# Two row-tiled matmul streams in one gated two-layer network: the upper stream's second products first, both streams started and ended together

## The chip, the core and the metric

The kernel runs on one core of one Trainium2 chip. The metric is the device time of one execution in microseconds (us). TensorE is called PE in the profile (its weight loads PEld), VectorE DVE, ScalarE ACT, GpSimd POOL, and the queue that issues most transfers SP.

## The reference

A causal 7-tap convolution with softmaxed taps for each of 8 heads is followed by two layers `x @ w_in`, a gate, `@ w_out`. All is float32; there are 8192 tokens, 192 features and 2048 hidden features.

```python
w = exp(weight - max); w = w / (sum(w) + 1e-9)               # 8 heads x 7 taps
x = conv(x, w)                                              # (2, 4096, 192) -> (8192, 192)
h = x @ w_in1;  x = (h * clip(h + 3, 0, 6) / 6) @ w_out1     # layer 0, (192, 2048), (2048, 192)
h = x @ w_in2;  out = where(h > 0, h, exp(min(h, 0)) - 1) @ w_out2   # layer 1
```

## The kernel before

**Blocks and slots.** The tokens are cut into 16 blocks of 512 (256 of each of the two batch rows), features and hidden features lie on partitions, and tokens run along the free axis. One slot `(l, b, f)` is layer `l`, block `b` and 128 of the 2048 hidden features, so a block has 16 slots in a layer and the kernel 512. The list `slots` fixes their order: blocks 0 and 1 of layer 0 woven into each other, blocks 2 to 6 of layer 0, then a block of layer 1 and a block of layer 0 in turn (nine of each), and at the end blocks 9 to 15 of layer 1 alone.

**A slot's work.** `mm1` makes the first products `h = w_in.T @ x` in PSUM (tile `h`, pool `ps_h` with three banks). `gate` reads `h`: in layer 0 ACT writes `u = relu(h + 3)` and DVE `g = min(u, 6) * h`; in layer 1 ACT writes `u = relu(-h)` and `u = exp(-u)`, and DVE `g = max(u - 1, h)`. `split_g` makes a high part `gh` (ACT) and a low part `gl = g - gh` (DVE). `mm2` makes the second products, which add to two accumulators of the block, `p0` and `p1`: high weights by `gh` and low weights by `gh` into `p0`, both at once into `p1`, then both with `gl`, five products in all. ACT and DVE take a slot in the order `u`, (`exp`,) `gh` of the slot before, and `g`, `gl` of the slot before (`first_done`), then side work: `run_jobs` steps through the convolution of later blocks, the preparation of weights and the stores, spread by costs and due times.

**Two streams.** The first 36 slots (`BOTH + LAG`) run first products on all 128 rows of the array. After that each product is cut in two: the lower 64 rows (`LO`) and the upper 64 rows (`UP`) of the contraction are two products in two row tiles of the array, which run at the same time. `stream(half, ...)` writes the two instruction lists, and a loop takes one instruction of each in turn. In each stream slot `s` has its first products (five or four, alternating) and then the five second products of slot `s - 4` (`LAG`). The lower stream is 8 instructions ahead (`BEHIND`): `h` is begun by the lower stream and ended by the upper one, and a tiny GpSimd write (`relay`) tells the upper that the lower has left the bank. So 8 lower products run alone at the start, and 8 upper ones at the end. Slots 32 to 511 have split second products, slots 36 to 511 split first products.

**Accumulators.** Each stream has its own `p0` and `p1`, so four of the five banks of `ps_o` are in use within a block, and the next block begins with one free bank. Where a block's lower products end, ACT copies them out (`lower_sum`: `y0`, `s1`), which frees their banks; where its upper ones end, DVE adds them to that (`upper_sum`, `job`). At such an end `stream` gives out the gate of the upper stream's slot after the first DVE sum. The last block is summed, transposed on PE and stored by `last_store`; `finish` orders its second products so that the last slot's come last.

Of the kernel before, what the change touches and what calls it, by code (L numbers as in the profile page):

```python
# [8 lines left out]
F32 = mybir.dt.float32  # L9
# [4 lines left out]
ALU = mybir.AluOpType  # L14
# [2 lines left out]

P = 128
LAG = 4
BEHIND = 8  # L20
PAUSE = 2
RA = 7
STAG = 2
LEAD = 1
# [5 lines left out]
NB = 512  # L30
HB = NB // 2
# [24 lines left out]
def conv_moe_moe2(ctx: ExitStack, tc: tile.TileContext, x, weight, w_in1, w_out1, w_in2, w_out2, out):  # L56
# [18 lines left out]
    B, S, D = x.shape  # L75
# [3 lines left out]
    NF = FF // P  # L79
# [6 lines left out]
    NBLK = NT // NB  # L86
# [267 lines left out]

    rests = {}

    def lower_sum(l, b, lower):

        k = SIXTH if l == 0 else 1.0
        if l == 0:  # L360
            y0 = yp.tile([P, NB], F32, name="y0", tag="y0")
        else:
            y2 = stage.tile([P, 2 * NB], F32, name="y2", tag="raw")
            y0, spare[b] = y2[:, 0:NB], y2[:, NB:2 * NB]
        s1 = tmp.tile([P, NB], F32, name="s1", tag="s1", bufs=1)
        pairs = [(y0, lower[0]), (s1, lower[1])]
        for y, p in reversed(pairs) if l == 1 and b == NBLK - 1 else pairs:
            act.mul(y, p, k)
        return y0, s1

    def upper_sum(l, b, upper, y0, s1):


        k = SIXTH if l == 0 else 1.0
        if l == 1 and b == NBLK - 1:
            spare.pop(b)
            yield from last_store(b, upper, y0, s1)
            return
        if upper is None:
            yield  # L380
        else:
            for i, y in enumerate((y0, s1)):
                vec.scalar_tensor_tensor(out=y, in0=upper[i], scalar=k, in1=y, op0=ALU.mult, op1=ALU.add)
                yield LATER if i else None
        h, other = (UP, LO) if l == 0 and b % 2 else (LO, UP)
        if l == 0:
            if b % 2 == 0:
                rests[b // 2] = yp.tile([P, NB], F32, name="yr", tag="yr", bufs=(RA + 1) // 2)
            yr = rests[b // 2]
        else:  # L390
            yr = spare.pop(b)
            out0 = store(b, 0, y0)
            next(out0)
        act.copy(yr[h], s1[other])
        if l == 1:
            yield from out0
        yield LATER
        vec.tensor_tensor(out=yr[h], in0=s1[h], in1=yr[h], op=ALU.add)
        yield
        if l == 1:  # L400
            yield from store(b, 1, yr)
        else:
            ys[b] = y0, yr
# [16 lines left out]

    zs = {}

    def last_store(b, upper, y0, s1):

        JB = B * JT // 2
        h = JB // B
        z = stage.tile([P, 2 * NB], F32, name="z", tag="raw")[:, 0:JB * D].rearrange("p (j d) -> p j d", d=D)

        def add(y, up, k0, k1):
            c = slice(k0 * HB, k1 * HB)  # L430
            vec.scalar_tensor_tensor(out=y[:, c], in0=up[:, c], scalar=1.0, in1=y[:, c], op0=ALU.mult, op1=ALU.add)

        def turn(y, js):
            ps = ps_h.tile([P, len(js), P], F32, name="pso", tag="h")
            for i, j in enumerate(js):
                nc.tensor.transpose(ps[:, i], y[:, j * P:(j + 1) * P], ident)  # L436
            return ps

        add(s1, upper[1], 0, B)
        add(y0, upper[0], 0, 1)  # L440
        add(y0, upper[0], 1, B)
        pr = turn(s1, range(JB))
        low = tmp.tile([P, JB, D - P], F32, name="low", tag="g")
        act.copy(low, pr[:, :, D - P:P])
        vec.tensor_tensor(out=z[:, :, P:D], in0=pr[:, :, 0:D - P], in1=low, op=ALU.add)
        for k, queue in enumerate((nc.sync, nc.scalar)):
            js = range(k * h, (k + 1) * h)
            pm = turn(y0, js)
            act.copy(z[:, k * h:(k + 1) * h, 0:P], pm)
            rows = slice(k * S + b * HB, k * S + (b + 1) * HB)  # L450
            queue.dma_start(out[rows].rearrange("(j p) d -> p j d", p=P), z[:, k * h:(k + 1) * h])
        yield

    def split_y(b):
        y0, yr = ys.pop(b)
# [61 lines left out]

    acc = {}

    def mm2(s, half, which=range(5), cols=slice(0, NB)):  # L520

        l, b, f = slots[s]
        gh, gl = gs[s]
        w = wo[l][half, f, :]
        first, last = f == 0, f == NF - 1
        if first:
            acc[l, b, half is UP] = [ps_o.tile([P, NB], F32, name=f"p{i}", tag="po") for i in range(2)]
        p0, p1 = acc[l, b, half is UP]
        w0h, wr, w0l = (w[:, k * P:(k + 1) * P] for k in range(3))
        todo = [(p0, w0h, gh, 0), (p0, w0l, gh, 0), (p1, wr, gh, 0), (p0, w0h, gl, 1), (p1, wr, gl, 1)]  # L530
        for i in which:
            p, k, m, end = todo[i]
            n = R + 2 if k is wr and end and not last else P
            nc.tensor.matmul(p[:n, cols], k[:, :n], m[half, cols], start=first and not end and k is not w0l,  # L534
                             stop=last and end == 1 and cols.stop == NB)
            yield


# [23 lines left out]
    def job(gen, n, a, e, work=0):  # L562

        jobs.append([e if callable(e) else lambda: e, a, gen, n, 0, work, 0, 0, -1])
# [47 lines left out]
    def whole(*gens):  # L612
        for g in gens:
            yield from g

    def drain(gen):
        for _ in gen:
            pass

    def due(item):  # L620
        kind, l, a, e = item
        return at[l, 0, a] + (LAG if kind == "out" else 0)

    def when(i):

# [115 lines left out]
    def first_done(s):  # L741
        if s == NS - 1:
            split(s - 1)
        raw_g[s] = gate(slots[s][0], hs.pop(s))
        split(s if s == NS - 1 else s - 1)
        run_jobs(s)

    def second_done(s, half):
        l, b, f = slots[s]
        if half is not LO:  # L750
            gs.pop(s)
        if f == NF - 1:
            if half is not UP:
                sums[l, b] = lower_sum(l, b, acc.pop((l, b, False)))
            if half is not LO:
                ev = upper_sum(l, b, acc.pop((l, b, True), None), *sums.pop((l, b)))
                next(ev)
                if s == NS - 1:
                    drain(ev)
                else:  # L760
                    now = min(s + LAG, NS - 1)
                    job(ev, 4 + 3 * l, now, now + 8, WORK["sum", l])

    sums = {}
    BOTH = at[0, 2, 0]

    def stream(half, slots1, behind):

        for s in slots1:
            if s < NS:  # L770
                yield from mm1(s, half)
            ends = s >= behind and half is UP and slots[s - LAG][2] == NF - 1
            if s < NS and half is not LO and not ends:
                first_done(s)
            if s >= behind:
                yield from mm2(s - LAG, half)
                second_done(s - LAG, half)
            if s < NS and ends:
                first_done(s)

    def finish(half):

        for s in range(NS - LAG, NS - 2):
            yield from mm2(s, half)
            second_done(s, half)
        s, e = NS - 2, NS - 1
        if half is LO:
            yield from mm2(s, half)
            for _ in range(PAUSE):
                yield  # L790
            yield from mm2(e, half, (2, 0, 4, 1, 3))
        else:
            yield from mm2(s, half, (2, 4))
            yield from mm2(e, half, (2, 4))
            yield from mm2(s, half, (0, 1, 3))
            for k in range(B):
                yield from mm2(e, half, (0, 1, 3), slice(k * HB, (k + 1) * HB))
        second_done(s, half)
        second_done(e, half)

    drain(stream(ALL, range(BOTH + LAG), LAG))
    with tc.manual_schedule():
        ends = {}
        n = {LO: 0, UP: BEHIND}
        for half in (LO, UP):
            for s in range(BOTH + LAG, NS + LAG):
                first = 5 if (half is LO) == (slots[s % NS][2] % 2 == 0) else 4
                if s < NS:
                    assert half is LO or n[half] > ends[s]
                    n[half] += first  # L810
                    ends[s] = n[half]
                n[half] += 5
        lower, upper = (whole(stream(half, range(BOTH + LAG, NS), LAG), finish(half)) for half in (LO, UP))
        for _ in range(BEHIND):
            next(lower)
        going = [lower, upper]
        while going:
            for g in list(going):
                if next(g, jobs) is jobs:
                    going.remove(g)  # L820
        run_jobs(NS + 9)


# [28 lines left out]
```

## Time and profile before

| | |
|---|---|
| Time, median of 3 runs | 1141.78 us (1141.73 to 1141.92) |
| The profiled execution | 1142.41 us, of which the span from the first to the last instruction is 1140.7 us |
| PE busy | 1131.0 us (99%) |
| DVE, ACT busy | 919.8 us (81%), 930.1 us (82%) |
| PE's granted clock | 0.999 of full speed |

The span is what an engine's instructions cover; 1.7 us of the profiled execution lie around it. Busy time of PE is that of modelled ends, so what counts below are the starts of its products and the gaps between them.

### The profile page before, as it was taken

Reading aid. Unit: us, or ns where it says so; the run is one execution under the profiler, and the core shown is the slowest. Engines: PE = TensorE matmul, PEld = TensorE weight load, DVE = VectorE, ACT = ScalarE, POOL = GpSimd, SP = SyncE. Lnnn points to the kernel's source line nnn. Section 1 sums busy time; section 2 is a strip of 40 time slices with the busy share of each in tenths; the row PEclk is TensorE's granted clock in tenths of the full one; section 3 lists DMA queues with packets and bytes.
Section 4 is the critical chain, followed back from the end, with each engine's and each line's share of the span. In section 5 each row is a group of like instructions: output and inputs, shape, how many; then the busy total and the mean of one; then the engine's idle time right before and its main releaser. Section 6 shows DMA issues by size and latency. Waiting matters only on the chain.

```text
span 1140.7 us, 25120 instructions
## 1 busy us (share of the span) xinstructions
PE 1131.0 (99%) x9507; PEld 991.5 (87%) x9507; DVE 919.8 (81%) x1560; ACT 930.1 (82%) x1685; POOL 45.0 (4%) x490
## 2 busy tenths in 40 slices
PE   8999999999999999999999999999999999999998
PEld 6788998988888999999888888888888888899997
DVE  7997999988887868778687787878867667777775
ACT  6877777788878787887878878787886888998896
POOL 0000000000000000000000000000000000000000
PEclk9999999999999999999999999999999999999999
DMA  6422012010010100101001010100000000000001
GB/s 184 112 58 51 24 43 47 29 29 1 2 28 2 25 5 2 29 1 29 2 11 20 1 29 1 20 11 1 15 2 15 2 6 10 15 15 16 13 5 26
DMA packets 105370, 26.80 MB, mean 23 GB/s; under 512 B 96416, under 2 KB 104096, under 8 KB 105248
## 3 DMA queue, kind: packets, MB, share of 16 engines
q1 hardware_dynamic: 104960, 24.99, 10.3%
q8 instruction: 74, 1.21, 0.5%
q14 instruction: 48, 0.39, 0.1%
q10 hardware_dynamic: 288, 0.20, 0.1%
HBM read 18.87 MB, written 6.29 MB: 22 GB/s over the span
## 4 chain that ended last, share of the span: by engine, by line
PE 97%; DVE 1%; ACT 1%; DMA 0%; issue 0%; SPq 0%; ACTq 0%
PE p L534 51%; PE h L491 46%; DMA raw<-in_moe_w_in_dram 0%; DVE acc L50 0%; DVE xw L50 0%; ACT u L50 0%; DVE wi0r L50 0%; ACT opC L50 0%; ACT xw L50 0%; DVE cw L50 0%; DVE wo L50 0%; ACT gh L50 0%; ACT opD L50 0%; PE pso L436 0%; SPq L239 0%
## 5 line engine op out<-in xcount | busy, mean ns | idle before, releaser
L534 PE MATMUL p<-gh,wo 64*128 64x512 f32 (+1 forms) x2978 | 570.8, 386 | 0.0
L50 DVE SCALAR_TENSOR_TENSOR g<-u,h 128x512 f32<-128x512 f32 x512 | 349.9, 683 | 185.7 <-ACT u L50 181.8
L534 PE MATMUL p<-gl,wo 64*128 64x512 f32 (+3 forms) x1985 | 453.9, 386 | 0.0
L534 PEld LDWEIGHTS p<-gh,wo 64*128 64x128 f32 (+1 forms) x2978 | 413.4, 184 | 38.8 <-ACT gh L50 0.2
L50 DVE TENSOR_TENSOR gl<-g,gh 128x512 fp32r<-128x512 f32 x512 | 350.2, 684 | 2.9 <-ACT gh L50 2.4
L50 ACT CAST gh<-g 128x512 fp32r<-128x512 f32 x512 | 311.4, 608 | 13.3 <-DVE g L50 13.0
L534 PEld LDWEIGHTS p<-gl,wo 64*128 64x128 f32 (+2 forms) x1985 | 274.5, 160 | 30.8 <-DVE gl L50 0.4
L50 ACT ACTIVATE u<-h,three 128x512 f32<-128x512 f32 x256 | 176.2, 689 | 108.2 <-PE h L491 105.5
L50 ACT ACTIVATE u<-h 128x512 f32<-128x512 f32 x256 | 152.5, 596 | 57.9 <-PE h L491 57.0
L50 ACT ACTIVATE u<-u 128x512 f32<-128x512 f32 x256 | 161.9, 632 | 8.1
L491 PE MATMUL h<-opA,wi0h 64*128 64x512 f32 (+1 forms) x476 | 166.9, 388 | 0.4 <-DVE g L50 0.2
L491 PE MATMUL h<-opB,wi0h 64*128 64x512 f32 (+1 forms) x476 | 166.6, 387 | 0.0
L491 PE MATMUL h<-opA,wi0l 64*128 64x512 f32 (+1 forms) x476 | 166.5, 387 | 0.0
L491 PE MATMUL h<-opA,wi1h 64*128 64x512 f32 x512 | 163.1, 387 | 0.0
L491 PE MATMUL h<-opA,wi1l 64*128 64x512 f32 x512 | 163.0, 386 | 0.0
L491 PE MATMUL h<-opB,wi1h 64*128 64x512 f32 x512 | 162.8, 386 | 0.0
L491 PE MATMUL h<-opC,wi0r 64*128 64x512 f32 (+1 forms) x366 | 133.3, 387 | 0.6 <-ACT opC L50 0.6
L491 PE MATMUL h<-opD,wi0r 64*128 64x512 f32 (+1 forms) x366 | 133.1, 387 | 0.0
L491 PE MATMUL h<-opD,wi1r 64*128 64x512 f32 x384 | 131.4, 386 | 0.0
L491 PE MATMUL h<-opC,wi1r 64*128 64x512 f32 x384 | 131.4, 386 | 0.0
L50 DVE SCALAR_TENSOR_TENSOR acc<-xT,taps,acc 128x256 f32<-128x256 f32 (+1 forms) x180 | 106.3, 603 | 0.1
L491 PEld LDWEIGHTS h<-opB,wi1h 64*128 64x128 f32 x512 | 94.1, 184 | 6.9
(89 smaller groups left out, 1215.7 us busy)
## 6 DMA issues: line engine op xcount, KB each, us to landing
raw<-in_moe_w_out_dram SPq DMA_DIRECT2D x16, 384.0 KB, 3.1
out_dram<-z SPq DMA_DIRECT2D x180, 32.0 KB, 1.6
raw<-in_moe_w_in_dram SPq DMA_DIRECT2D x7, 512.0 KB, 3.8
x_sq<-in_x_dram SPq DMA_DIRECT2D x112, 32.0 KB, 2.2
raw<-in_moe_w_in_dram SPq DMA_DIRECT2D x8, 256.0 KB, 4.2
xr_sq<-in_x_dram SPq DMA_DIRECT2D x56, 32.0 KB, 2.2
x_sb<-in_x_dram SPq DMA_DIRECT2D x4, 128.0 KB, 3.6
raw<-in_moe_w_in_dram SPq DMA_DIRECT2D x4, 128.0 KB, 3.9
```

What stands on the lines that cost most here:

```text
L50: return fn(*args, **kw)
L491: mm = nc.tensor.matmul(h, k, m[half], start=low and i == 0, stop=high and i == len(todo) - 1)
L534: nc.tensor.matmul(p[:n, cols], k[:, :n], m[half, cols], start=first and not end and k is not w0l, stop=last and end == 1 and cols.stop == NB)
```

## The change

The streams' lists are written anew. The lower stream has `mm1(s)` and then `mm2(s - 5)` (`LAG2`), and none in its first turn; the upper stream begins with 8 second products (`HEAD`) and goes on in the same way. So the lower stream still leads by 8 in first products, and the upper one leads by 8 in second products. The five second products stand in the order `p0, p0, p0, p1, p1`.

The upper stream's accumulators are now those that ACT copies out (`first_sum`): `y0` after the third product, `s1` after the fifth. DVE's sums (`second_sum`) belong to the lower stream, `y0` after its third product. Side work of the slot whose gate comes just before a block's lower end is held back until after that end (`first_done`, `second_done`). At the end of the kernel the last slot's three products into `p0` run with all 128 rows, in two halves of 256 columns, after both streams; `last_store` copies the upper accumulators by ACT and adds the lower by DVE. Weights of the second layer's `w_out` are due one slot earlier.

```diff
-BEHIND = 8
-PAUSE = 2
+LAG2 = LAG + 1
+HEAD = 8
...
-    def lower_sum(l, b, lower):
+    def first_sum(l, b, accs):
...
+        act.mul(y0, accs[0], k)
+        yield y0, s1
+        act.mul(s1, accs[1], k)
+        yield
...
-        add(s1, upper[1], 0, B)
-        add(y0, upper[0], 0, 1)
-        add(y0, upper[0], 1, B)
+        act.copy(s1, two[1])
+        act.copy(y0, two[0])
+        add(s1, 1, 0, B)
+        add(y0, 0, 0, 1)
+        add(y0, 0, 1, B)
...
-    def mm2(s, half, which=range(5), cols=slice(0, NB)):
+    def mm2(s, half, which=(0, 1, 3, 2, 4), cols=slice(0, NB)):
...
-        return at[l, 0, a] + (LAG if kind == "out" else 0)
+        return at[l, 0, a] + ((LAG, LAG2 - 2)[l] if kind == "out" else 0)
...
-        run_jobs(s)
+        if s < BOTH + LAG or s + 1 >= NS or slots[s + 1 - LAG2][2] < NF - 1:
+            run_jobs(s)
+
+    def main_done(s, half):
+        l, b, f = slots[s]
+        if f < NF - 1:
+            return
+        if half is not LO:
+            firsts[l, b] = first_sum(l, b, acc.pop((l, b, half is UP)))
+            sums[l, b] = next(firsts[l, b])
+        if half is LO:
+            seconds_of[l, b] = second_sum(l, b, acc.pop((l, b, False)), *sums.pop((l, b)))
+            next(seconds_of[l, b])
 
     def second_done(s, half):
         l, b, f = slots[s]
+        if half is not UP:
+            gs.pop(s)
+        if f < NF - 1:
+            return
         if half is not LO:
...
+            next(firsts.pop((l, b)))
...
+        if half is not UP:
+            now = min(s + (LAG if half is ALL else LAG2), NS - 1)
+            job(seconds_of.pop((l, b)), 4 + 3 * l, now, now + 8, WORK["sum", l])
+            if half is LO:
+                run_jobs(now - 1)
...
+    def seconds_with(s, half):
+
+        for i, _ in enumerate(mm2(s, half)):
+            if i == 2:
+                main_done(s, half)
+            if i == 4:
+                second_done(s, half)
+            yield
+
+    def seconds(half):
+
+        for s in range(BOTH, NS - 2):
+            yield from seconds_with(s, half)
         s, e = NS - 2, NS - 1
...
+        yield from mm2(s, half, (2, 4))
+        yield from mm2(e, half, (2,))
+        yield from mm2(s, half, (0, 1))
+        yield from mm2(e, half, (4,))
+        yield from mm2(s, half, (3,))
         second_done(s, half)
...
+    def lower_rows():
+
+        two = seconds(LO)
+        for s in range(BOTH + LAG, NS):
+            yield from mm1(s, LO)
+            if s >= BOTH + LAG2:
+                yield from some(two, 5)
+        yield from two
+
+    def upper_rows():
+
+        two = seconds(UP)
+        yield from some(two, HEAD)
+        for s in range(BOTH + LAG, NS):
+            yield from mm1(s, UP)
+            first_done(s)
+            if s >= BOTH + LAG2:
+                yield from some(two, 5)
+        yield from two
...
+        for k in range(B):
+            drain(mm2(NS - 1, ALL, (0, 1, 3), slice(k * HB, (k + 1) * HB)))
+        last_store(NBLK - 1, *(acc.pop((1, NBLK - 1, up)) for up in (False, True)))
         run_jobs(NS + 9)
```

Three places show the new order. The names in the rows carry the buffers' numbers, which differ between the two programs.

PE where the streams begin (behind the last full-row product, `p1_526`), before: `h_1197` is slot 36's, and the second tile `h_1197` in a row with a lower tile between belongs to the upper stream.

```order
L534 MATMUL p1_526<-gl_1110,wo0_96 128x512
L491 MATMUL h_1197<-opA_668,wi0h_90 128x512
L491 MATMUL h_1197<-opB_669,wi0h_90 128x512
L491 MATMUL h_1197<-opA_668,wi0l_91 128x512
L491 MATMUL h_1197<-opC_670,wi0r_92 128x512
L491 MATMUL h_1197<-opD_671,wi0r_92 128x512
L534 MATMUL p0_1204<-gh_1136,wo0_96 128x512 x2
L534 MATMUL p1_1205<-gh_1136,wo0_96 128x512
L534 MATMUL p0_1204<-gl_1138,wo0_96 128x512
L491 MATMUL h_1197<-opA_668,wi0h_90 128x512
```

And after the change:

```order
L534 MATMUL p1_526<-gl_1110,wo0_96 128x512
L491 MATMUL h_1197<-opA_668,wi0h_90 128x512
L534 MATMUL p0_1199<-gh_1138,wo0_96 128x512
L491 MATMUL h_1197<-opB_669,wi0h_90 128x512
L534 MATMUL p0_1199<-gh_1138,wo0_96 128x512
L491 MATMUL h_1197<-opA_668,wi0l_91 128x512
L534 MATMUL p0_1199<-gl_1140,wo0_96 128x512
L491 MATMUL h_1197<-opC_670,wi0r_92 128x512
L534 MATMUL p1_1200<-gh_1138,wo0_96 128x512
```

Eight upper second products have moved between the lower stream's first rows; upper first products still begin 8 rounds after the lower ones.

DVE at the end of block 8 of layer 0, whose gates are already layer 1's, before: `y0_8094` is the sum of the upper `p0` (then freed), `g` and `gl` are gates of slots that run on.

```order
L50 SCALAR_TENSOR_TENSOR g_8071<-u_8072,h_8034 128x512
L50 TENSOR_TENSOR gl_8078<-g_8042,gh_8076 128x512
L50 SCALAR_TENSOR_TENSOR y0_8094<-p0_7615,y0_8094 128x512
L50 SCALAR_TENSOR_TENSOR g_8120<-u_8121,h_8065 128x512
L50 TENSOR_TENSOR gl_8127<-g_8071,gh_8125 128x512
```

And after the change, where `y0_8088` is the sum of the lower `p0`:

```order
L50 SCALAR_TENSOR_TENSOR g_8069<-u_8070,h_8032 128x512
L50 TENSOR_TENSOR gl_8076<-g_8040,gh_8074 128x512
L50 SCALAR_TENSOR_TENSOR g_8103<-u_8104,h_8063 128x512
L50 TENSOR_TENSOR gl_8110<-g_8069,gh_8108 128x512
L50 SCALAR_TENSOR_TENSOR y0_8088<-p0_7616,y0_8088 128x512
```

The sum that frees a bank has moved from ahead of the gate of slot e+4 (e is the block's last slot) to behind it.

PE at the same end, after the change, from the last upper first product of slot e+4 (`h_8063`) to the first lower product that needs the bank freed by that sum (`p1_8150`); of the rows between, those of the upper `p0_8118` and of `h` are left out.

```order
L491 MATMUL h_8063<-opD_7750,wi1r_95 128x512
...
L534 MATMUL p0_7616<-gl_8016,wo0_96 128x512
...
L534 MATMUL p1_7617<-gl_8016,wo0_96 128x512
...
L534 MATMUL p0_8149<-gh_8045,wo1_97 128x512
...
L534 MATMUL p1_8150<-gh_8045,wo1_97 128x512
```

`p0_8149` is the 12th lower product behind the round of the first row and needs the bank that ACT's `s1` copy frees; `p1_8150` is the 15th. Before the change it was the upper `p1` that needed DVE's sum, and the lower `p1` that needed ACT's copy `y0`.

## Rows read from the trace of the kernel before

**Rows 1.** The page: the chain that ended last, shares by engine.

```profile
PE 97%; DVE 1%; ACT 1%; DMA 0%; issue 0%; SPq 0%; ACTq 0%
```

**Rows 2.** That chain in order of time: start us, us, what.

```profile
709.97 1.13 PE h L491 x10
711.10 1.13 PE p L534 x10
...
715.41 1.13 PE p L534 x10
```

**Rows 3.** Waits: engine, line, waited for, us in total, times, longest.

```profile
PEld h L491 <- DVE g L50: 2.1, 7, 0.6
...
PEld p L534 <- ACT y L50: 0.2, 1, 0.2
```

**Rows 4.** Timeline, streams' begin: start, us, engine, line, operation, tiles, shapes, [idle before].

```profile
101.04 0.49 PE L491 MATMUL h<-opA,wi0h 64*128 64x512 f32 x1
...
102.66 0.50 PE L491 MATMUL h<-opA,wi0h 64*128 64x512 f32 x1
```

**Rows 5.** Timeline, the kernel's end.

```profile
1128.37 0.39 PE L491 MATMUL h<-opD,wi1r 64*128 64x512 f32 x1
...
1131.08 0.62 ACT L50 CAST gh<-g 128x512 fp32r<-128x512 f32 x1 [0.76 <-DVE g L50]
...
1133.93 0.40 PE L534 MATMUL p<-gh,wo 64*128 64x256 f32 x2
...
1134.53 0.28 PE L534 MATMUL p<-gl,wo 64*128 64x256 f32 x1
1134.74 0.42 PEld L436 LDWEIGHTS pso<-ident,s 128*128 128x128 f32 x4
...
1135.86 0.70 ACT L50 COPY z<-pso 128x256 f32<-128x256 f32 x2
...
1136.59 0.42 ACTq L451 DMA_DIRECT2D out_dram<-z  x1
```

**Rows 6.** Timeline around 31 us, full rows.

```profile
29.94 0.86 PE L534 MATMUL p<-gh,wo 128*128 128x512 f32 x3
...
30.65 0.69 DVE L50 TENSOR_TENSOR gl<-g,gh 128x512 fp32r<-128x512 f32 x1
...
31.42 0.19 PEld L491 LDWEIGHTS h<-opC,wi0r 128*128 128x128 f32 x1 [1.06 <-ACT opC L50]
```

**Rows 7.** Timeline, a block's end with layer 1's gates.

```profile
618.01 0.39 PE L491 MATMUL h<-opD,wi1r 64*128 64x512 f32 x1
...
618.20 0.60 ACT L50 ACTIVATE u<-h 128x512 f32<-128x512 f32 x1 [0.27 <-PE h L491]
...
618.83 0.63 ACT L50 ACTIVATE u<-u 128x512 f32<-128x512 f32 x1
...
619.37 0.60 ACT L50 CAST gh<-g 128x512 fp32r<-128x512 f32 x1
619.49 0.69 DVE L50 SCALAR_TENSOR_TENSOR g<-u,h 128x512 f32<-128x512 f32 x1 [0.75 <-ACT u L50]
619.87 0.59 ACT L50 ACTIVATE y<-p 128x512 f32<-128x512 f32 x1
620.10 0.69 DVE L50 TENSOR_TENSOR gl<-g,gh 128x512 fp32r<-128x512 f32 x1
620.36 0.59 ACT L50 ACTIVATE s<-p 128x512 f32<-128x512 f32 x1
...
621.44 0.69 DVE L50 SCALAR_TENSOR_TENSOR y<-p,y 128x512 f32<-128x512 f32 x1 [0.66 <-ACT u L50]
```

**Rows 8.** Timeline, a first product that waits for a gate.

```profile
187.01 0.68 DVE L50 SCALAR_TENSOR_TENSOR g<-u,h 128x512 f32<-128x512 f32 x1
...
187.44 0.39 PE L491 MATMUL h<-opB,wi0h 64*128 64x512 f32 x1
...
187.75 0.49 PE L491 MATMUL h<-opA,wi0h 64*128 64x512 f32 x1
...
188.09 0.39 PE L491 MATMUL h<-opB,wi0h 64*128 64x512 f32 x1
```

**Rows 9.** Timeline, weights' preparation on ACT.

```profile
276.71 0.61 ACT L50 CAST gh<-g 128x512 fp32r<-128x512 f32 x1
277.22 0.51 ACT L50 CAST wo<-xw 128x384 fp32r<-128x384 f32 x1
277.63 0.55 ACT L50 ACTIVATE xw<-raw 128x384 f32<-128x384 f32 x1
278.08 0.59 ACT L50 ACTIVATE u<-h 128x512 f32<-128x512 f32 x1
```

More of the change, by code (lines that the diff above doesn't have):

```diff
@@ L365, in lower_sum, with second_sum @@
         s1 = tmp.tile([P, NB], F32, name="s1", tag="s1", bufs=1)
[L366 to L371, printed above, removed]
-        k = SIXTH if l == 0 else 1.0
[L375 to L379, printed above, removed]
+        act.mul(y0, accs[0], k)
+        yield y0, s1
+        act.mul(s1, accs[1], k)
+        yield
+    def second_sum(l, b, accs, y0, s1):
+        k = SIXTH if l == 0 else 1.0
+        if accs is None:
             yield
@@ L382, in upper_sum @@
             for i, y in enumerate((y0, s1)):
-                vec.scalar_tensor_tensor(out=y, in0=upper[i], scalar=k, in1=y, op0=ALU.mult, op1=ALU.add)
+                vec.scalar_tensor_tensor(out=y, in0=accs[i], scalar=k, in1=y, op0=ALU.mult, op1=ALU.add)
                 yield LATER if i else None
@@ L421, in conv_moe_moe2, with last_store @@
     zs = {}
-    def last_store(b, upper, y0, s1):
+    def last_store(b, one, two):
         JB = B * JT // 2
@@ L427, in last_store, with add @@
         z = stage.tile([P, 2 * NB], F32, name="z", tag="raw")[:, 0:JB * D].rearrange("p (j d) -> p j d", d=D)
-        def add(y, up, k0, k1):
+        y0 = yp.tile([P, NB], F32, name="y0", tag="y0")
+        s1 = tmp.tile([P, NB], F32, name="s1", tag="s1", bufs=1)
+        def add(y, i, k0, k1):
             c = slice(k0 * HB, k1 * HB)
-            vec.scalar_tensor_tensor(out=y[:, c], in0=up[:, c], scalar=1.0, in1=y[:, c], op0=ALU.mult, op1=ALU.add)
+            vec.tensor_tensor(out=y[:, c], in0=one[i][:, c], in1=y[:, c], op=ALU.add)
         def turn(y, js):
@@ L451, in last_store @@
             queue.dma_start(out[rows].rearrange("(j p) d -> p j d", p=P), z[:, k * h:(k + 1) * h])
-        yield
     def split_y(b):
@@ L534, in mm2 @@
             nc.tensor.matmul(p[:n, cols], k[:, :n], m[half, cols], start=first and not end and k is not w0l,
-                             stop=last and end == 1 and cols.stop == NB)
+                             stop=end == 1 and (last and cols.stop == NB or s == NS - 2 and half is UP and p is p0))
             yield
@@ L748, in second_done @@
     def second_done(s, half):
         l, b, f = slots[s]
+        if half is not UP:
+            gs.pop(s)
+        if f < NF - 1:
+            return
         if half is not LO:
[L751 to L762, printed above, removed]
+            next(firsts.pop((l, b)))
@@ L764, in conv_moe_moe2 @@
+        if half is ALL:
+            seconds_of[l, b] = second_sum(l, b, None, *sums.pop((l, b)))
+            next(seconds_of[l, b])
+        if half is not UP:
[3 more added lines that the diff above has]
+                run_jobs(now - 1)
+    firsts = {}
+    seconds_of = {}
     sums = {}
     BOTH = at[0, 2, 0]
[L767 to L785, printed above, removed]
-        s, e = NS - 2, NS - 1
[L787 to L797, printed above, removed]
-        second_done(s, half)
-        second_done(e, half)
@@ L801, in conv_moe_moe2, with whole_rows @@
-    drain(stream(ALL, range(BOTH + LAG), LAG))
+    def whole_rows():
+        for s in range(BOTH + LAG):
+            yield from mm1(s, ALL)
+            first_done(s)
+            if s >= LAG:
+                yield from seconds_with(s - LAG, ALL)
+    def seconds_with(s, half):
[8 more added lines that the diff above has]
+            yield from seconds_with(s, half)
+        s, e = NS - 2, NS - 1
+        yield from mm2(s, half, (2, 4))
[3 more added lines that the diff above has]
+        yield from mm2(s, half, (3,))
+        second_done(s, half)
@@ new lines, in some @@
+    def some(gen, n):
+        for _ in range(n):
+            next(gen)
+            yield
+    def lower_rows():
[10 more added lines that the diff above has]
+            yield from mm1(s, UP)
+            first_done(s)
+            if s >= BOTH + LAG2:
+                yield from some(two, 5)
+        yield from two
@@ L802, in conv_moe_moe2 @@
+    drain(whole_rows())
     with tc.manual_schedule():
         ends = {}
-        n = {LO: 0, UP: BEHIND}
+        n = {LO: 0, UP: HEAD}
         for half in (LO, UP):
[L806 to L810, printed above, removed]
-                    ends[s] = n[half]
-                n[half] += 5
-        lower, upper = (whole(stream(half, range(BOTH + LAG, NS), LAG), finish(half)) for half in (LO, UP))
@@ L814, in conv_moe_moe2 @@
-        for _ in range(BEHIND):
-            next(lower)
-        going = [lower, upper]
+            for s in range(BOTH + LAG, NS):
+                assert half is LO or n[half] > ends[s]
+                n[half] += 5 if (half is LO) == (slots[s][2] % 2 == 0) else 4
+                if half is LO:
+                    ends[s] = n[half]
+                n[half] += 5 * (s >= BOTH + LAG2)
+        going = [lower_rows(), upper_rows()]
         while going:
```

## The prediction, made before the changed kernel ran

> **What bounds the kernel now.** I read the chain that ended last first: PE holds 97% of it [rows 1], so only what PE executes, or is kept from executing, counts; copies, gates and sums matter where they make PE wait. The chain in order of time then gives PE's unit. Two neighbouring slots take ten first-product rounds less one (five and four) and ten second-product rounds, 19 in all, a round being one lower and one upper product that run together; they take 711.10 to 715.41, 4.31 us, so a round is 0.2267 us [rows 2]. Streams' length: 476 slots with 4.5 first products on average and 480 with five second ones are 4,542 rounds, and the 8 lower products alone at the start make 4,550, by 0.2267 1031.3 us. The timeline has the first split product at 101.04 and the last start at 1134.53 [rows 4, 5], 1033.5 us. So about 2.2 us in 1141 are waits inside the streams, and the rest is products. The view of waits agrees: seven waits of first products for `g` make 2.1 us (partly ahead of the streams), and one second product waits 0.2 for ACT's `y` [rows 3]. Reading single stalls in the timeline I find four within the streams (that of `y` and three of `g`), each 0.20 to 0.23 us. With this much already tight the change can gain only where it cuts rounds, and can lose wherever an end of a block becomes late by more than a fraction of a round.
>
> **What a late release costs.** In the `g` wait, DVE's `g` starts at 187.01 and lasts 0.68, so it ends at 187.69; PE's first product starts at 187.75, 0.06 later, and the next product of the stream stands at 188.09, 0.34 behind it in place of 0.23 [rows 8]. So what PE waits for must be done 0.06 + 0.11 = 0.17 us before a product is due, and each later microsecond is lost by both streams, since they go through PE in one order.
>
> **Fewer rounds: the two streams begin together.** Eight upper second products stand beside the eight lower first products that ran alone. Slot 511's last upper first product therefore comes after five second rounds fewer (slot 32's five; the other three are of slot 33, and are paid back as lag): 5 x 0.2267 = **-1.13 us**.
>
> **The end.** From that product, at 1128.37, to the last store's issue at 1136.59 is 8.22 now [rows 5]. After the change 19 rounds follow it (slot 510's and 511's seconds that are left, in both streams): 4.31; then the change from half rows to all rows, which no row shows and which I take at 0.1 on top of one round (0.23), between nothing and 0.3; then six full-row products on 256 columns, of which five starts at 0.12 count (1133.93 to 1134.53 has such products so spaced [rows 5]): last start at 4.31 + 0.33 + 0.60 = 5.24. From the last start to the store's issue it was 1136.59 - 1134.53 = 2.06 [rows 5], and 5.24 + 2.06 = 7.30; since ACT's `y0` copy now ends at about 5.4 and three DVE adds of 0.69 and two halves follow it, I take 7.5: **-0.72**. The last gate could hold this up: `gh` of slot 511 ended 1131.08 + 0.62 - 1128.37 = 3.33 after the last first product [rows 5], and `gl`, which reads it and lasts 0.69, not before 4.02; in the new order their first products are the 15th and the 18th round behind it, due at 3.40 and 4.08, so both are near the edge, 0.1 to 0.15 over with the 0.17 that PE takes to restart (worked out above); but `u` of that slot stood behind a `gh` in the trace, and `gh` now comes from an earlier turn. I count no stall, and 0.3 in the range.
>
> **The start.** At 31 us the full-row products wait 1.06 us for ACT's `opC` [rows 6]. In the order `p0, p0, p0, p1, p1` the third `p0` product needs `gl`, which DVE ends at 31.34; before, it was the fourth, with a `p1` ahead of it. One product more is thus left to do behind the wait: **+0.2**.
>
> **The stalls of now.** The one for ACT's `y` goes, since the copy now stands ahead of side work: **-0.2**. The other three are late `g` tiles where side work falls between gates; side work is still there, and I count them as recurring, with 0.7 either way in the range.
>
> **Ends of blocks.** Here is where waits are added. The streams have 29 ends of a block ahead of the last; the 13 whose gates (slot e+4's, e the block's last) are layer 0's have no `exp`, and I find them in time by more than 0.4. Sixteen have layer 1's gates. The new order on DVE puts the `y0` sum, which frees a bank of the lower stream, behind the gate of slot e+4. Durations from a block's end of now [rows 7], counted from the last upper first product of that slot (618.01 there): `u` starts 0.20 later, `exp` 0.63 after it, `g` 0.66 after `exp`, `gl` 0.61 after `g`, the `y0` sum I put the same 0.60 after `gl`, and it lasts 0.69: 0.20 + 0.63 + 0.66 + 0.61 + 0.60 + 0.69 = 3.39. With 0.17 to get PE under way that is 3.56. The lower product which needs that bank is the fifteenth behind the same mark: 15 x 0.2267 = 3.40. So it comes **0.16 late, at each such end**. The old order had the sum ahead of that gate, and what it freed was the upper `p1`; the trace has no such wait between 301 and 1119 us.
>
> The other freed bank: ACT's `s1` copy stands behind `u`, `exp` and `gh`, that is 0.20 + 0.63 + 0.54 + 0.50 to its start and 0.59 to its end, 2.46 [rows 7], with 0.17 2.63; the twelfth product needs it at 12 x 0.2267 = 2.72. It is in time by 0.09 and I count nothing, but it is the tightest thing that I count at nothing.
>
> Fifteen of the sixteen ends have no side work on ACT and DVE in the slots before: 15 x 0.16 = **+2.4**. One, the end of block 6 of layer 0, has ACT's preparation of weights (`wo`, then `xw`) between `gh` of slot e+2 and the `y0` copy. From `gh` to what follows it is 0.51, then `wo` to `xw` 0.41 and `xw` to the next 0.45 [rows 9], so these two put 0.86 more on ACT, of which the slack there takes 0.13; `u` of slot e+4 comes 0.73 late. Then the `s1` product waits 0.73 - 0.09, about 0.65, and the sum, of whose 0.73 + 0.16 the first wait has absorbed 0.65, another 0.24: **+0.9** (from nothing, if the work has been done earlier, to 1.2).
>
> A rule of the Trainium skill bears on the chain: "ScalarE: Activation LUTs", under "What ACT_TABLE_LOAD costs", has it that back-to-back activations overlap by about 93 ns. The trace agrees where the second does not read the first's result (0.54 and 0.50 apart at a duration of 0.60 [rows 7]), and not for `exp` behind `u`, 0.63 apart. If that pair too overlapped, the chain would be 0.12 shorter by an estimate from that page, fifteen ends would cost 0.6 in place of 2.4, and the sum below would be -0.4.
>
> **Sum.** -1.13 - 0.72 + 0.2 - 0.2 + 2.4 + 0.9 = +1.45 us, on a span of 1140.7 a span of 1142.15. The profiled execution took 1142.41, 1.7 more than its span, so 1143.9; the median of the runs, 1141.78, lies 0.63 below that execution, and I expect a median of 1143.2. The two parts that I am sure of (a gain of 1.13, and ends that were easy and now are tight) are of opposite sign and like size; the whole is inside 0.2% (2.3 us, about what measurement of this kernel tells from no change), between 1139.5 and 1144.06.
>
> **Rivals.**
> - *The sum is not late.* If the `y0` sum ends in time (DVE or ACT run 0.16 ahead of what I put down, or PE's queue of started products takes up a late bank), nothing is lost at ends, and if all four stalls and block 6's also go, the median is 1141.78 - 1.13 - 0.72 + 0.2 - 0.8 = 1139.3. For it: 0.16 is less than a round, and the sum's step of 0.60 behind `gl` is worked out and not seen. Against: the stagger of 0.60 to 0.66 stands in the rows of the end [rows 7], and a late tile of 0.02 did cost PE time in [rows 8]. It decides at a chain shorter by 0.16. Chance 0.1.
> - *The overlap between dependent activations* or another shortening of 0.1 us or so per end: 1141.4. Against it every `u` to `exp` step of the trace is 0.62 to 0.63. Chance 0.05.
> - *The `s1` copy is late too.* It has 0.09 to spare. If ACT is 0.2 to 0.3 later at an end (the `y0` copy, now ahead of `u`, delays `u` of slot e+4), the twelfth product waits 0.1 to 0.2 at all 16 ends, and the fifteenth its 0.16 beside that, since ACT's lateness is carried into `g` and the sum: 16 x 0.2 more, 1146.4. For it: the copy starts 0.50 behind `gh` of slot e+2, whose place is 0.9 before the mark, so it ends near +0.2, just where `u` is due. Against: ACT's next starts 0.1 before its former one has ended, so `u` at +0.20 holds. It decides at 0.09 us. Chance 0.16.
> - *The ends do not cost this, but side work does*: held back until after the lower end it falls in a bunch on the following gates and makes more late `g` tiles of 0.2: with seven of them and no loss from the sum, 1142 to 1143.5. It ends inside the likeliest one's range; chance 0.1.
>
> **How the numbers follow.** My forecast has 0.59 and its own range is 1141.6 to 1144.8: the loss per end between 0.05 and 0.23 (a whole round; 0.8 to 3.4), block 6 between 0 and 1.2, late `g` 0.7 either way. The range over the cases leaves out the outer half of the first rival and most of the third: 1139.4 to 1145.4. Faster by over 0.2% is half of the first rival and a corner of the forecast, 0.09; slower by over 0.2% is the third rival and a sixth of the forecast (0.1), 0.26; within it 0.65.
>
> **What the changed trace would show.** Right: second products of the lower stream waiting for DVE's `y` some fifteen times, with 0.3 or so of idle each, and gaps of 0.16 in PE's rounds at ends from 301 us on; no such wait at ends with layer 0's gates; one wait for ACT's `s` at the end of block 6; upper products in pairs from the first 101 us on; no wait for ACT's `y` near 172; the last upper first product 1.1 earlier when the losses are taken out, and 7.5 from it to the last store. Wrong: no waits for `y` (the first rival), waits for `s` at all ends (the third), waits for `g` in place of both (the fourth), or a gap of several tenths where the array goes from half rows to all rows.

## The result and the profile after

The changed kernel takes 1151.51 us (median of 6 runs, 1151.31 to 1151.86) beside 1141.85 for the kernel before (6 runs): a ratio of 1.0084, 95% interval 1.0074 to 1.0095, 9.7 us slower. The profiled span is 1149.6, 8.9 more than before.

PE still holds the end, but less exclusively than in [rows 1]. The page's chain that ended last, after:

```profile
PE 93%; ACT 4%; DVE 2%; issue 1%; DMA 0%; SPq 0%; ACTq 0%; DVEq 0%
```

ACT has risen from one per cent to four and DVE from one to two. The view of waits names where; its columns are total us, times, longest:

```profile
PEld p L534 <- DVE y L50: 7.8, 19, 0.9
PEld p L534 <- ACT s L50: 6.0, 17, 1.0
PEld h L491 <- DVE g L50: 3.9, 7, 1.2
...
PE h L491 <- DVE g L50: 1.3, 4, 0.8
```

Of these only `h <- g` stood in [rows 3], with 2.1. The one wait for ACT's `y` there is gone. Nineteen weight loads of second products now wait for DVE's `y`, and seventeen for ACT's `s`. The idle time of a waiting load is not what PE loses (0.33 and 0.39 us at the end shown below, where the starts of PE's products fall back by 0.43 in all); what is lost is read from counts. A table by stretch gives PE's products (in the first bracket): after,

```profile
101.00:304.00 203.00, 200.76 (x1745) 171.06 (x1746) 183.58 (x329) 160.59 (x300) 8.13 (x92) 1.00 0.12 29
304.00:1130.00 826.00, 826.00 (x7227) 754.30 (x7225) 635.35 (x1026) 682.05 (x1214) 33.45 (x380) 1.00 0.07 12
```

and before:

```profile
101.00:302.00 201.00, 201.00 (x1753) 177.64 (x1754) 184.00 (x330) 161.77 (x302) 8.45 (x92) 1.00 0.12 29
302.00:1119.00 817.00, 817.00 (x7210) 721.61 (x7208) 633.45 (x1023) 678.60 (x1211) 33.99 (x380) 1.00 0.07 12
```

A product costs half a round, 0.1133 us (0.2267 / 2). Before, 7,210 of them account for all 817 us. After, 7,227 account for 819.1 of 826: **6.9 us lost**, although PE's busy column says 826.00 in 826 (a busy PE is not a PE at its peak, and here only the count shows it). Ahead of that, 1,745 account for 197.8 of 203, 5.2 lost, beside 2.3 of 201 before, of which 0.9 belonged to the eight products that ran alone: 3.8 more now. The engine's granted clock is 1.00 in all four lines, 2.4 GHz.

One end of a block after the change, timeline, counted from the upper stream's last first product at 624.80:

```profile
624.80 0.39 PE L491 MATMUL h<-opD,wi1r 64*128 64x512 f32 x1
...
625.21 0.39 PE L491 MATMUL h<-opD,wi1r 64*128 64x512 f32 x1
625.22 0.60 ACT L50 ACTIVATE u<-h 128x512 f32<-128x512 f32 x1
...
625.71 0.09 POOL L493 MEMSET relay<- 1x1 f32 x1 [2.18 <-PE p L534]
625.85 0.63 ACT L50 ACTIVATE u<-u 128x512 f32<-128x512 f32 x1
626.39 0.60 ACT L50 CAST gh<-g 128x512 fp32r<-128x512 f32 x1
626.51 0.69 DVE L50 SCALAR_TENSOR_TENSOR g<-u,h 128x512 f32<-128x512 f32 x1 [0.98 <-ACT u L50]
626.90 0.59 ACT L50 ACTIVATE s<-p 128x512 f32<-128x512 f32 x1
627.12 0.68 DVE L50 TENSOR_TENSOR gl<-g,gh 128x512 fp32r<-128x512 f32 x1
...
627.54 0.30 PEld L534 LDWEIGHTS p<-gh,wo 64*128 64x128 f32 x4 [0.33 <-ACT s L50]
627.72 0.68 DVE L50 SCALAR_TENSOR_TENSOR y<-p,y 128x512 f32<-128x512 f32 x1
...
628.46 0.18 PEld L534 LDWEIGHTS p<-gh,wo 64*128 64x128 f32 x1 [0.39 <-DVE y L50]
```

Every step of the chain has its predicted length (`u` to `exp` 0.63, to `g` 0.66, to `gl` 0.61, to the sum 0.60, 0.68 long), but `u` starts **0.42** after the mark, not 0.20. The `s1` copy ends 2.69 after it (2.46 predicted), the `y0` sum 3.60 (3.39 predicted). With 0.17 to restart, the copy is 0.14 later than the twelfth product is due, 2.72, and the sum 0.37 later than the fifteenth, 3.40.

Where the 0.22 was lost is seen in the kernel before. The prediction took the product at 618.01 [rows 7] for the upper stream's last. These two rows of the same timeline stood around it:

```profile
617.77 0.39 PE L491 MATMUL h<-opC,wi1r 64*128 64x512 f32 x1
...
618.52 0.09 POOL L493 MEMSET relay<- 1x1 f32 x1 [1.95 <-PE h L491]
```

The `relay` write, which follows the lower stream's last first product of a slot, comes 0.51 after 618.01 (and 0.50 after 625.21 above). So 618.01 is the lower stream's; nor could `u`, which starts at 618.20 [rows 7], read the result of a product that runs to 618.40. The upper stream's last one started at 617.77, one round sooner, and `u` is 0.43 behind that, of which 0.39 is the product itself. Rounds were counted from one product and microseconds from the other.

The start of the streams has waits that the kernel before had not. Timeline after:

```profile
112.05 1.39 DVE L50 TENSOR_TENSOR wi1r<-xw,wi1r 64x512 fp32r<-64x512 f32 x2
113.47 0.69 DVE L50 SCALAR_TENSOR_TENSOR g<-u,h 128x512 f32<-128x512 f32 x1
...
114.21 0.50 PE L491 MATMUL h<-opA,wi0h 64*128 64x512 f32 x1 [0.77 <-DVE g L50]
```

Weight preparation of 1.39 lies ahead of a `g`, and the first product that needs the bank of its `h` waits. In the kernel before, the same preparation stood one gate later, behind this `g`:

```profile
112.82 0.68 DVE L50 SCALAR_TENSOR_TENSOR g<-u,h 128x512 f32<-128x512 f32 x1
...
114.14 1.39 DVE L50 TENSOR_TENSOR wi1r<-xw,wi1r 64x512 fp32r<-64x512 f32 x2
```

And the end, timeline after:

```profile
1138.23 0.39 PE L491 MATMUL h<-opD,wi1r 64*128 64x512 f32 x1
...
1143.69 0.28 PE L534 MATMUL p<-gl,wo 128*128 128x256 f32 x1
...
1145.93 0.44 ACTq L452 DMA_DIRECT2D out_dram<-z  x1
```

From the last upper first product to the last store's issue it is 7.70, where [rows 5] had 8.22.

### The profile page after: what moved, and what is told of

The parts are those of the page before. It is cut to its first block, busy times and chain, and to the rows that moved or that the text cites. A ratio compares the mean times of both kernels' runs of the same rounds, so it can differ in the third digit from the quotient of the medians.

```text
span 1149.6 us, 25134 instructions
## 1 busy us (share of the span) xinstructions
PE 1136.7 (99%) x9504; PEld 1014.7 (88%) x9504; DVE 920.2 (80%) x1560; ACT 931.9 (81%) x1685; POOL 44.1 (4%) x490
## 4 chain that ended last, share of the span: by engine, by line
PE 93%; ACT 4%; DVE 2%; issue 1%; DMA 0%; SPq 0%; ACTq 0%; DVEq 0%
PE p L534 49%; PE h L491 44%; ACT u L50 1%; ACT gh L50 1%; DVE acc L50 0%; DMA raw<-in_moe_w_in_dram 0%; DVE g L50 0%; ACT opC L50 0%; DVE gl L50 0%; ACT opD L50 0%; DVE xw L50 0%; DVE wi1r L50 0%; ACT xw L50 0%; DVE wi0r L50 0%; DVE cw L50 0%
## 5 line engine op out<-in xcount | busy, mean ns | idle before, releaser
L534 PE MATMUL p<-gh,wo 64*128 64x512 f32 (+1 forms) x2976 | 709.3, 388 | 1.1 <-ACT s L50 0.6
L534 PE MATMUL p<-gl,wo 64*128 64x512 f32 (+2 forms) x1984 | 596.3, 386 | 0.0
L534 PEld LDWEIGHTS p<-gl,wo 64*128 64x128 f32 (+2 forms) x1984 | 252.5, 160 | 19.5 <-DVE gl L50 0.2
L491 PE MATMUL h<-opA,wi1h 64*128 64x512 f32 x512 | 196.5, 391 | 0.0
L491 PE MATMUL h<-opA,wi1l 64*128 64x512 f32 x512 | 194.1, 387 | 0.0
L491 PE MATMUL h<-opB,wi1h 64*128 64x512 f32 x512 | 194.1, 387 | 0.0
L491 PE MATMUL h<-opA,wi0h 64*128 64x512 f32 (+1 forms) x476 | 181.5, 389 | 1.6 <-DVE g L50 1.3
L491 PE MATMUL h<-opC,wi1r 64*128 64x512 f32 x384 | 146.4, 386 | 0.0
L491 PE MATMUL h<-opD,wi1r 64*128 64x512 f32 x384 | 146.3, 386 | 0.0
L491 PEld LDWEIGHTS h<-opA,wi1h 64*128 64x128 f32 x512 | 94.2, 184 | 4.8 <-DVE g L50 0.2
```

Source lines behind the costliest of these rows:

```text
L491: mm = nc.tensor.matmul(h, k, m[half], start=low and i == 0, stop=high and i == len(todo) - 1)
```

## The experiments

Each compared with the kernel before, run beside it on the same chip (medians 1141.7 to 1142.0). All of them compute the whole reference.

**The gate of slot e+4 behind the upper stream's second products.** The changed kernel, with

```diff
             yield from mm1(s, UP)
-            first_done(s)
+            ends = s >= BOTH + LAG2 and slots[s - LAG][2] == NF - 1
+            if not ends:
+                first_done(s)
             if s >= BOTH + LAG2:
                 yield from some(two, 5)
+            if ends:
+                first_done(s)
```

> At a block's end the gate of the upper stream's slot is given out after its five second products in place of before them, so ACT's s1 copy and DVE's y0 sum stand ahead of u, exp, gh and of g, gl. Theory: both banks come free in time at all ends: -6.4 at the sixteen and -1.5 at earlier ones; g of that slot comes 0.75 later, and its bank is needed 0.3 after that, so it costs nothing: about 1144 us. Rival one (the gate is then the late one): second-product waits go but first products wait for g at the ends, 1147 to 1152. Rival two (the pairing or the side work costs the time): 1150 to 1152 with other waits in the same places.

Measured 1143.57 us, ratio 1.0013 (1.0005 to 1.0022): 7.9 us of the 9.7 are back. No second product waits for `y` or `s` any more, and nothing is lost behind 304 us; what is left are waits for `g`. The waits of this kernel, and its stretch:

```profile
PEld h L491 <- DVE g L50: 5.8, 12, 1.2
```

```profile
304.00:1120.00 816.00, 816.00 (x7201) 781.55 (x7199) 632.94 (x1023) 678.12 (x1210) 33.72 (x378) 1.00 0.07 12
```

7,201 products at half a round are 816.1 of 816. The second rival falls: the pairing of the streams and the side work are as they were. The first holds only in small: waits for `g` rose from 3.9 to 5.8 us, all of the new ones ahead of 304 us.

**Only DVE's part of the gate moved.** ACT's `u`, `exp`, `gh` keep their place (`act_part`); `g` and `gl` follow the five second products.

```diff
-            first_done(s)
+            if ends:
+                part = act_part(s)
+            else:
+                first_done(s)
             if s >= BOTH + LAG2:
                 yield from some(two, 5)
+            if ends:
+                dve_part(s, *part)
```

> At a block's end only DVE's part of the gate (g, and gl of the slot before) is moved behind the upper stream's five second products; ACT keeps the order of the changed kernel (u, exp, gh, s1). Theory (the copy is 0.16 late and the sum 0.24 more): the waits for DVE's y go at all ends, those for ACT's s stay at the sixteen with layer 1's gates, 0.16 each, and at the end of block 6, 0.8: 3.3 above the run with the whole gate moved, 1146.5 us. Rival (the sum alone costs it all, and the copy's wait is only there because both come together): 1143.5.

Measured 1147.98 (1.0053, 1.0039 to 1.0066). The waits for `y` are gone, those for `s` are what they were:

```profile
PEld p L534 <- ACT s L50: 6.0, 17, 1.0
```

```profile
304.00:1130.00 826.00, 826.00 (x7257) 745.75 (x7255) 636.20 (x1029) 684.77 (x1219) 33.63 (x382) 1.00 0.07 12
```

7,257 products are 822.5 of 826: 3.5 lost, 0.23 at each of the fifteen ends with layer 1's gates in this stretch (the sixteenth, block 6's, lies ahead of it), where I had 0.16; the time is 1.5 above my 1146.5. So of the 6.9 the late copy alone costs 3.5, and the late sum, coming behind it, another 3.4. What the sum would cost with the copy in time was not run.

**The gate between the copy and the sum.** The gate after two of the five, so that `s1` is ahead of it and the sum behind:

```diff
             if s >= BOTH + LAG2:
-                yield from some(two, 5)
+                yield from some(two, 2)
+                if ends:
+                    first_done(s)
+                yield from some(two, 3)
```

> The gate is given out after two of the upper stream's five second products, behind the s1 copy and ahead of the y0 sum. Theory: ACT starts s1 0.87 after the last upper first product, u 1.37, exp 2.0, g 2.66, gl 3.27, the y0 sum 3.87 to 4.56; with 0.17 to restart that is 1.33 behind the fifteenth product's 3.40, 0.93 more than the 0.40 of now at sixteen ends (15 us), and without exp 0.75 at thirteen ends with layer 0's gates (10 us), which lose little now: about 1176 us, all in waits of second products for DVE's y, none for ACT's s. Rival (the copy's place decides): faster than the changed kernel, 1149 or less.

Measured 1175.63 (1.0295, 1.0281 to 1.0309), within 0.4 of the working. Every one of the 29 ends waits for `y`, none for `s`:

```profile
PEld p L534 <- DVE y L50: 35.8, 29, 1.8
PE p L534 <- DVE y L50: 23.6, 29, 1.3
```

```profile
354.27 0.68 DVE L50 SCALAR_TENSOR_TENSOR y<-p,y 128x512 f32<-128x512 f32 x1
...
355.01 0.49 PE L534 MATMUL p<-gh,wo 64*128 64x512 f32 x1 [1.06 <-DVE y L50]
```

The sum ends at 354.95 and the product is there 0.06 later, as in [rows 8].

**The same in the kernel before.** There the `ends` clause gave out the gate behind the first sum; here it is taken out.

```diff
-            ends = s >= behind and half is UP and slots[s - LAG][2] == NF - 1
+            ends = False
```

> The kernel before with one thing undone: at a block's end the gate of the upper stream's slot is given out ahead of its second products and of DVE's y0 sum, as everywhere else. Theory (the same chain in the other kernel): u starts 0.80 after the last upper first product (behind both copies), exp 0.63, g 0.66, gl 0.61, the sum 0.60 on and 0.69 long, 3.99, with 0.17 to restart 4.16; the upper p1 that needs its bank is the twelfth product, 2.72 after the same mark. 1.44 late at sixteen ends, and without exp 0.86 at thirteen: 34 us, 1176 us, in waits of second products for DVE's y. Rival (the late bank is a matter of which stream's accumulators ACT copies out, and of the streams' new begin, so the place of the sum alone does little here): 1142 to 1147.

Measured 1179.96 (1.0341, 1.0327 to 1.0355), 38 us where I had 34. The waits that are new:

```profile
PEld p L534 <- DVE y L50: 41.1, 29, 2.4
PE p L534 <- DVE y L50: 28.9, 29, 1.9
```

The kernel before depends on that clause; the change wrote the streams anew without it.

**A longer head of the upper stream**, nine and ten second products.

```diff
-HEAD = 8
+HEAD = 10
```

> Nine second products ahead. Theory: one round, 0.23 us, more for both banks: the copy is in time, the sum still 0.17 late in place of 0.40, so sixteen ends give back 0.23 each, 3.7: about 1147.7 us. Rival: 1150 to 1152.

> The upper stream begins with ten second products in place of eight. Theory (a clean end of a block loses 0.40 us because ACT's s1 copy and DVE's y0 sum come 0.16 and 0.40 later than the lower stream's twelfth and fifteenth product need them, both counted from the upper stream's own last first product): the lower stream needs both banks two rounds, 0.45 us, later against that mark, so the waits at the sixteen ends with layer 1's gates go, -6.4, and about 0.8 at earlier ends; at the kernel's end gl of slot 511 is needed two rounds sooner, +0.5. About 1145 us. Rival (the row tiles' new pairing, or side work bunched behind the ends, costs the time): between 1150 and 1152, since neither is touched.

Measured 1157.73 (1.0138, 1.0124 to 1.0152) and 1172.27 (1.0266, 1.0252 to 1.028): slower, where I expected faster, by an error of sign. `HEAD` also holds back the upper stream's first products by as many rounds, so the gate, and with it the chain, comes later against the lower stream: the bank is asked for one and two rounds sooner after the mark. Put right after the fact, it is with ten 0.37 + 0.45 at the sum, and 0.42 more since `u` starts 0.84 after the mark, with both copies ahead of it: 1.24 at an end. Timeline of one end with ten:

```profile
351.83 0.59 ACT L50 ACTIVATE y<-p 128x512 f32<-128x512 f32 x1
...
351.96 0.39 PE L491 MATMUL h<-opD,wi1r 64*128 64x512 f32 x2
...
352.32 0.59 ACT L50 ACTIVATE s<-p 128x512 f32<-128x512 f32 x1
...
352.80 0.60 ACT L50 ACTIVATE u<-h 128x512 f32<-128x512 f32 x1
...
356.04 0.50 PE L534 MATMUL p<-gh,wo 64*128 64x512 f32 x2 [0.97 <-DVE y L50]
```

That the cost follows this count was worked out behind the result, so it supports the theory less than the runs above; the rival (nothing changes) falls.

**Side work not held back** at ends:

```diff
-        if s < BOTH + LAG or s + 1 >= NS or slots[s + 1 - LAG2][2] < NF - 1:
-            run_jobs(s)
+        run_jobs(s)
...
-            if half is LO:
-                run_jobs(now - 1)
```

> The side work of the slot before a lower end is not held back: it is stepped through behind each gate as in the kernel before. Theory (late copies and sums at ends whose slots have no side work at all): the sixteen ends stay as they are; earlier ones move by 1 either way: 1150.5 to 1153. Rival (bunching after the hold makes late g tiles, which the 2.5 us lost ahead of 301 us are): 1148.5 to 1149.5.

Measured 1157.69 (1.0138, 1.0124 to 1.0151): both expectations missed. With the hold 19 weight loads wait for `y`, without it

```profile
PEld p L534 <- DVE y L50: 15.2, 28, 2.0
PEld p L534 <- ACT s L50: 5.9, 17, 1.1
```

28. I had said that ends with layer 0's gates are in time by 0.4; without the hold, side work stands between their gate and the sum and they are late too. With the hold they have far less than 0.4 to spare. The end at 385 us in the changed kernel:

```profile
384.28 0.68 DVE L50 SCALAR_TENSOR_TENSOR y<-p,y 128x512 f32<-128x512 f32 x1
...
385.25 0.39 PE L534 MATMUL p<-gh,wo 64*128 64x512 f32 x1
```

The sum ends 0.29 ahead of its product, of which PE needs 0.17. So the hold, one part of the change, is worth 6 us in it, and is no cause of the loss at ends; the waits at 111 and 114 us stand without it too.

**The order of the five products alone**, in the kernel before:

```diff
-    def mm2(s, half, which=range(5), cols=slice(0, NB)):
+    def mm2(s, half, which=(0, 1, 3, 2, 4), cols=slice(0, NB)):
```

> The kernel before with its five second products in the order p0, p0, p0, p1, p1 and nothing else. Theory (the order as such costs nothing; what costs is when banks come free): 1141.7 to 1142.5 us, the same. Rival (gl is asked for one product sooner, or the weights' sequence of this order is slower): 1143 or more, with waits for gl.

Measured 1141.82, ratio 1.0 (0.9991 to 1.0008): nothing.

**No side work behind the streams' first two gates**, on top of the moved gate:

```diff
-        if s < BOTH + LAG or s + 1 >= NS or slots[s + 1 - LAG2][2] < NF - 1:
+        if s not in (BOTH + LAG, BOTH + LAG + 1) and (s < BOTH + LAG or s + 1 >= NS or slots[s + 1 - LAG2][2] < NF - 1):
```

> As the run with the whole gate moved, and no side work behind the gates of the first two slots of the streams (36 and 37). Theory (the streams' begin brings slot 37's and later gates 1.13 us sooner, and side work of 1.8 us on ACT and 1.9 on DVE at 105 to 113 us is then in their way; 1.4 us of waits at 111 and 114): these waits shrink to 0.3 or less and some of the work comes in the way later: 1142.3 us. Rival (side work only moves the same wait to another slot): 1143.5.

Measured 1142.61 (1.0005, 0.9996 to 1.0014). The waits at 111 and 114 us are gone; one of 0.9 has come at 117.55 and one for `y` of about 1 at 209. A net 1.0 is gained. A table by stretch shows how little room there is behind (DVE's busy time is the third number with a bracket):

```profile
120.00:160.00 40.00, 40.00 (x355) 38.81 (x353) 38.98 (x71) 32.40 (x62) 1.59 (x19) 1.00 0.10 28
160.00:200.00 40.00, 40.00 (x353) 35.18 (x351) 38.74 (x71) 31.49 (x61) 1.68 (x19) 1.00 0.25 54
```

DVE is busy for 97% there, so it is likely that work held back at one place is in the way at the next; that is argued, not shown. The kernel before has nearly the same, 96 and 95%, and loses little:

```profile
120.00:160.00 40.00, 40.00 (x356) 36.07 (x354) 38.31 (x70) 32.51 (x63) 1.83 (x18) 1.00 0.13 35
160.00:200.00 40.00, 40.00 (x352) 34.19 (x350) 38.04 (x67) 31.42 (x60) 1.62 (x18) 1.00 0.20 43
```

So a full DVE alone does not make a wait; where side work falls between the gates counts too.

**A finer step of side work.** The two subtractions of `wi1r` in steps of their own, in three kernels:

```diff
                 vec.tensor_tensor(out=r[o, k], in0=f[h], in1=r[h, k].bitcast(F32), op=ALU.subtract)
+                if l == 1 and k == 0:
+                    yield
```

> As the run with the whole gate moved, and the second layer's w_in remainder (wi1r), whose two DVE subtractions of 0.69 stood in one step of the side work, in two steps. Theory (between 100 and 220 us DVE is busy for 93 to 100% and a step of 1.39 between two gates is what makes g late): the wait of 1.0 at 114 us shrinks by 0.5 to 0.7, 1142.9 us. Rival (DVE has no room there whatever the steps): 1143.3 to 1144.

> The same two steps in the kernel without side work behind the streams' first two gates. Theory: its waits at 117 and 209 us, 0.9 each behind a step of 1.39, shrink by 0.6 each: 1141.4 us, 0.4 below the kernel before. Rival (no room): 1142.3 to 1143.

> The same two steps in the kernel before. Both theories: it has no wait behind such a step of over 0.2 us, so 1141.5 to 1142.2, the same.

Measured 1145.86 (1.0036, 1.0022 to 1.0049), 1145.36 (1.0032, 1.0019 to 1.0045) and 1144.41 (1.0023, 1.0014 to 1.0033): 2.3 to 2.8 slower each, and in the kernel before too, where I expected nothing. Waits for `g` in the kernel with the gate moved, and in the kernel before:

```profile
PEld h L493 <- DVE g L50: 8.2, 14, 1.3
```

```profile
PEld h L493 <- DVE g L50: 4.5, 7, 1.1
```

They were 5.8 and 2.1. The wait behind `wi1r` shrank at 113 us, and others came at 157 to 163 and 229 to 234. The edit also changes the count of steps by which `run_jobs` spreads all later preparation, so it does not tell the step's length from the new spread; that stays open. No version here beats the kernel before.

## Why the prediction was wrong

- **Ends of blocks: the step that failed.** "Counted from the last upper first product of that slot (618.01 there)": that row was the lower stream's. The upper product is at 617.77, `u` is 0.42 behind it, and the chain's 3.56 is 3.78 against 3.40: 0.38 in place of 0.16. Measured, the fifteen ends behind 304 us lose 0.43 or so each by the starts of PE's products, 6.5 in place of 2.4; of 0.43, 0.05 stays without a reason.
- **The `s1` copy: counted at nothing, "in time by 0.09".** The same 0.22 makes it 0.14 late; measured 0.23 at an end where only the copy is late, 3.5 of the 6.9. Waits for `s`, expected at block 6's end alone, stand at all sixteen ends. The third rival had the copy late, but by another cause (the `y0` copy in front of `u`), and at 1146.4 too small.
- **Late waits for `y` as a mechanism: right.** The places (ends with layer 1's gates, from 301 us on), the bank and the number there, fifteen, were as worked out, and the place of the gate ahead of copy and sum is shown as the cause: gate behind both, 7.9 gained; only DVE's part of it behind the sum, the copy's half is left; sum still later, 1175.63 where 1176 was worked out.
- **Ends with layer 0's gates, "in time by more than 0.4".** Ten of the thirteen are in time, but by less: 0.12 at the one at 385 us, and most of the difference is the same round. At 210 and 245 us, where DVE has side work, the sum is late (1.1 lost by the starts of PE's products), and at 454 us too (0.35), where the reason is open. Moving the gate took these waits away as well.
- **Fewer rounds, -1.13: there, but not kept.** From the first split product to slot 511's last upper one it is 1037.25 in place of 1027.33 us: 9.92 more, of which 6.9 and 3.8 are the counted losses and -1.13 the rounds (9.6 in all; the rest stays open). Of the 3.8, 1.4 us is lost at 111 and 114 (by the starts of PE's products), and nothing of that was in the sum: late `g` tiles were put down as recurring, 0.7 either way. Two things differ there from the kernel before: the sooner rounds bring these gates sooner, and `wi1r` stands one gate earlier. Taking side work away behind the first two gates took the waits away; which of the two made them is open.
- **The end, -0.72: -0.52 measured**, with last start 5.46 after the mark in place of 5.24. The step from half rows to all rows, for which no row stood, came out as taken (0.32 in place of 0.33); about 0.1 went at `gh` of slot 511, counted as no stall, and 0.1 at the second full-row product. **The start, +0.2: did not come;** the first split product is at 100.98, 0.06 sooner than in [rows 4].
- **The stall for ACT's `y`: gone, as said.** Other waits for `g` recur and are larger (3.9 in place of 2.1).
- The rule of "ScalarE: Activation LUTs" in the Trainium skill ("What ACT_TABLE_LOAD costs"), that back-to-back activations overlap, is again not seen for `exp` behind `u`, 0.63 apart at the end shown. It was no part of the miss.

Terms of the sum as measured: fifteen ends behind 304 us 6.5, where 2.4 stood, and the one at 454 us 0.35; block 6's end 1.1 by the starts of products at 280 us, where 0.9 stood, a part of the 3.8 lost ahead of 304 us; the rest of that, 2.7 (1.4 at 111 and 114 us, 1.1 at the ends of 210 and 245 us), where nothing stood; rounds -1.13; end -0.52.

## What to carry to other kernels

Where two streams share a line of the code, find out which of them a row belongs to before counting rounds from it: an event that only one of them has (here the `relay` write) tells, and one round of 0.23 us at fifteen ends was the largest single part of this miss (3.3 of 8.3 us). A release that is in time by less than a round is not in time until start, chain and due product are counted from the same row. And before a few rounds are taken from a stretch, look whether the engine that feeds it (here DVE, 95 to 97% busy) has room for its deadlines to come sooner: here 1.13 us of rounds went with 1.4 us of new waits, though that the one brought the other is not shown.

## What the runs showed of the hardware

Little that was new: the durations of the chain of before came back to 0.01 us at the end shown after. At an end where only the copy was late PE lost 0.23, and where the sum behind it was late too, 0.43. PE's busy time showed none of it: 826.00 of 826 us with 6.9 lost.
